# Sparse attention into an ELU layer on one core: another order for the opening, and the second batch's pieces from a list

## The chip, the core and the metric

The kernel runs on one core of one Trainium2 chip. A core has five instruction streams that run beside each other and meet only at semaphores: TensorE (PE, the matmuls; its weight loads are shown as PEld), VectorE (DVE), ScalarE (ACT), GpSimd (POOL) and SyncE (SP). Each engine takes its own instructions in the order in which the program issued them, so a piece that waits holds up what stands behind it on that engine. The metric is the device time of one execution in microseconds (us).

## What is computed

There are 8 batches of 8 heads, 576 positions and 64 values per head. The first four heads use a local mask (a query sees itself and the 31 positions before it), the other four a strided mask (a query sees earlier positions of the same residue modulo 32). The attention output, 4608 tokens of 512 values, goes through a two-layer feed-forward block with an ELU between.

```python
scores = scale * np.matmul(q, k.transpose(0, 1, 3, 2))
mask_local = (rel >= 0) & (rel < stride)
mask_strided = (rel >= 0) & (pos[None, :] % stride == pos[:, None] % stride)
...
h = x @ w_in                                   # 4608x512 @ 512x2048
g = np.where(h > 0.0, h, alpha * (np.exp(np.minimum(h, 0.0)) - 1.0))
return (g @ w_out).astype(np.float32)          # 4608x2048 @ 2048x512
```

## The kernel before

**Two streams of work, interleaved.** The feed-forward block works on chunks of 512 tokens, nine in all; attention works on batches of 576 tokens. Chunk 0 needs batch 0, chunk 1 needs all of batches 0 and 1, and so on. So batch 0 is computed first and almost alone (the *opening*), and from then on attention of batch nb+1 is cut into small pieces which are put between the matmuls of chunk nb.

**Attention pieces.** A batch has four pairs of heads: `s0`, `s1` (strided) and `l0`, `l1` (local). Capital `S0`, `S1` in the opening's list are the strided pairs of batch 1. A `Pair` has these pieces:

- `t_q`, `t_k`: TensorE transposes of q and k into a PSUM bank (L368 strided, 5 matmuls; L382 local, 12), and one copy of the bank to SBUF (L371, L385).
- `s0`, `s1` (scores, first and second half, L500: 4 or 6 matmuls into the double bank `pair_a`), followed by an exponential on ScalarE (L508) that gives the probabilities `pr`. In batches above 0 the mask multiplication on VectorE (L523) is issued right behind it; in batch 0 it is a piece of its own, `m0`, `m1`.
- `v`: a copy of the strided values into the layout with a column of ones (L421, two instructions). `halo`: a copy of the last 32 rows of each local value block (L428).
- `a0`, `a1`: probabilities times values (L542), then a reciprocal (L550) and a product (L551) on VectorE, which give the rows of `x`.
- `x`: transposes of `x` (L578 strided, L591 local) and a copy into `xT` (L585 and L587, or L595), from which the feed-forward matmuls read.

**Which engine copies.** `Pair.copy` takes ScalarE for batches 0 and 1, except, in batch 0, the steps named in `ON_VECTOR`. The halo of batch 1 is on VectorE.

**The opening.** `OPENING` is an order written out by hand. `fill.n` means n matmuls of 512 columns into a bank that nobody reads (L724). `moe.c` runs one quarter of the contraction for the first three tiles of chunk 0 (L629), so these three tiles are ready when the chunk begins. The attention and feed-forward banks are shared out by `Ring`s: `pair_a` for scores, three single banks for transposes and `a` pieces, and three banks (two halves and `single3`) for the tiles of chunk 0.

**A chunk.** For each of 16 steps s the loop runs the pieces of gap 2s, four matmuls into a bank (`moe_in`, L629), the ELU (`moe_act`), the pieces of gap 2s+1, and then an output part (`moe_out`, L678, four matmuls; a finished output of 128 rows is copied at L683 and stored). The ELU is an exponential on ScalarE (L655) and two VectorE instructions (L662, then L664, which reads the bank); for the steps in `ON_SCALAR` (4, 7, 10, 13, 15) of chunk 0 it is the exponential, a Relu on ScalarE (L658) and one VectorE instruction (L659). A bank comes free for the next tile when L664, or the Relu, has read it. In this document m3 means the four matmuls of step 3 of chunk 0, and so on to m15.

**The gaps of batch 1.** `attention(b, start, pitch, at)` places the pieces by a start, a pitch from pair to pair and eight offsets. For batch 1 these are `(3, 6, (-3, -2, 0, 2, 4, 6, 9, 3))`: a pair begins every six gaps, its scores come at 0 and 2, `a0` and `a1` at 4 and 6, and `x` at 9. The output parts of chunk 0 come behind m11, m13 and m15.

**Loads.** All loads of inputs are issued by GpSimd in program order; `w_in` comes in four quarters (512 columns each, four steps of a chunk each), then `w_out` in four.

Of the kernel before, what the change touches and what calls it, by code (L numbers as in the profile page):

```python
# [32 lines left out]
PIECES = (-2, -1, 0, 2, 3, 5, 7, 0)  # L33
TIMES = (
# [4 lines left out]
    ((2, 8, 15, 22), 0, PIECES),  # L39
)  # L40

OPENING = """
s0.cast_q s0.t_q s0.t_k s1.cast_q s1.t_k s0.s0 s0.m0 s1.t_q s0.s1 s0.m1 fill.2 l0.t_q s1.s1
s1.m1 s1.s0 s1.m0 l0.t_k l1.t_q fill.1 s0.v l0.s0 l0.m0 l1.t_k l0.s1 s1.a0 s0.a0 l0.m1 l1.s0
s1.a1 s0.a1 fill.1 l1.s1 l1.m0 fill.1 s1.halo s1.x fill.1 s0.x l1.m1 fill.1 l0.a0 fill.1 l0.a1
l1.a0 moe.2 l1.a1 S0.t_q l0.x S1.t_q moe.3 l1.x moe.0 moe.1
""".split()  # L50
ON_VECTOR = "s0.t_q s1.cast_q s1.t_k l0.t_q s0.v l1.x".split()


ON_SCALAR = (4, 7, 10, 13, 15)
# [4 lines left out]
def kernel(  # L59
# [55 lines left out]
    def share(sc, hps, ops, ring):  # L115
        rings.update(sc=Ring(*sc), hps=Ring(*hps), ops=Ring(*ops), ring=Ring(*ring))
# [71 lines left out]
    def load_local(b, name):  # L188
        if name == "v":

            nc.gpsimd.dma_start(
                out=v_loc[b % 3][32:128, :, :, :D].rearrange("p h i d -> p (h i) d"),
                in_=v[b, 0:4].rearrange("h (i p) d -> p (h i) d", p=LB))
            return
        flat = nat[name, "loc"][b % 3]
        if b < EARLY:
            nc.gpsimd.dma_start(
                out=flat[0:LB].rearrange("p (h x) -> p h x", h=4),
                in_=src[name][b, 0:4].rearrange("h (p j) d -> p h (j d)", j=L_RUN))
            return  # L200
        t = flat[:, 0:20 * D].rearrange("p (a i e d) -> p a i e d", a=2, i=5, d=D)
        for h in range(4):
            nc.gpsimd.dma_start(  # L203
                out=t[:, h // 2, 0:4, h % 2],
                in_=src[name][b, h, 0:512].rearrange("(i p) d -> p i d", p=128))
        for a in range(2):
            nc.gpsimd.dma_start(
                out=t[0:64, a, 4],
                in_=src[name][b, 2 * a:2 * a + 2, 512:576].rearrange("h p d -> p h d"))

    def transpose_batch(b, local):

        def strided():
            for name, to in (("q", qT), ("k", kT)):
                nc.sync.dma_start_transpose(out=to["str"][b % 2],
                                            in_=nat[name, "str"][b % 3])

        if BY_DMA <= b <= LATE and local < 2:
            strided()
        if b >= EARLY and local:  # L220
            for name, to, o in (("q", qT, 0), ("k", kT, 32)):
                for a in range(2):
                    nc.sync.dma_start_transpose(
                        out=to["loc"][b % 2][:, a, o:o + 640].rearrange(
                            "p (i r) -> p i r", r=128),
                        in_=nat[name, "loc"][b % 3][:, 640 * a:640 * a + 640])
        if b > LATE:
            strided()

    def load_batch(b):  # L230
        for name in "qkv":
            load_strided(b, name)
        for name in "qkv":
            load_local(b, name)
# [87 lines left out]
    def load_w_in(i):  # L322
        nc.gpsimd.dma_start(out=w_in_sb[:, :, 512 * i:512 * (i + 1)],
                            in_=wi[:, :, 512 * i:512 * (i + 1)])
# [5 lines left out]
    load_strided(1, "v")  # L330
    load_local(1, "q")
    load_local(1, "k")
    load_local(1, "v")
    load_w_in(2)


    class Pair:
# [6 lines left out]

        def copy(self, step, late):

            if self.b == 0:
                late = f"{self.name}.{step}" in ON_VECTOR
            return nc.vector.tensor_copy if late else nc.scalar.copy

        def cast(self, name):
# [214 lines left out]
        def x_out(self):  # L566
# [22 lines left out]
            else:  # L589
# [4 lines left out]
                        identity[0:LB, 0:LB])  # L594
                self.copy("x", self.b > 1)(dst, xt[:, 0:S])  # L595

    def attention(b, start, pitch, at):


        gaps = {}  # L600
        pairs = [Pair(b, s, hp) for s in (b < LATE, b >= LATE) for hp in range(2)]
        begin = [start + pitch * i for i in range(4)] if pitch else start
        if b >= LATE:
            gaps[begin[0]] = [pairs[3].halo]
        for i, pr in enumerate(pairs):
            if b == 1 and pr.strided:
                pr.t_q = lambda: None
            for off, piece in ((at[0], pr.t_q), (at[1], pr.t_k),
                               (at[7], lambda pr=pr: pr.v_in(0)),
                               (at[7] + (b > 1), lambda pr=pr: pr.v_in(1)),  # L610
                               (at[2], lambda pr=pr: pr.scores(0)),
                               (at[3] if b < WHOLE else at[2] + (b < LATE),
                                lambda pr=pr: pr.scores(1)),
                               (at[4], lambda pr=pr: pr.av(0)),
                               (at[5] - (b >= LATE and i == 0),
                                lambda pr=pr: pr.av(1)),
                               (at[6] + (b > 1 and pr.strided) + (b >= LATE), pr.x_out), (at[5] - 2, pr.halo if b < LATE else lambda: None)):
                gaps.setdefault(begin[i] + off, []).append(piece)
        return gaps
# [85 lines left out]
    def range_flag(row_ok16):  # L705
        cnt = rings["ring"].next()
        nc.tensor.matmul(cnt[0:1, 0:1], lhsT=row_ok16, rhs=ones, start=True, stop=True)
        nc.vector.tensor_scalar(flag, cnt[0:1, 0:1], scalar1=127.5, scalar2=None,
                                op0=ALU.is_le)

    def run(gaps, keys):
        for gap in sorted(g for g in gaps if g in keys):
            for piece in gaps[gap]:
                piece()

    every = range(-10, 1000)
    pairs = {p.name: p for p in (Pair(0, s, hp) for s in (True, False) for hp in range(2))}
    pairs.update((f"S{hp}", Pair(1, True, hp)) for hp in range(2))
    parts = [s for s in OPENING if s.startswith("moe")]
    for step in OPENING:  # L720
        pair, what = step.split(".")
# [29 lines left out]
    def outs(nb, s):  # L751

        if nb == 0:
            return [(0, i) for i in range(3) if s == 11 + 2 * i]
        step = [(nb - 1, i) for i in range(3, MC)]
        if nb < n_chunks:
            step += [(nb, i) for i in range(3)]
        else:
            step[0:2] = step[1::-1]
        return step[s:s + 1]  # L760

    for nb in range(n_chunks + 1):

        if nb + 1 < B:
            gaps = attention(nb + 1, *TIMES[min(nb + 1, 4)])
            if nb == 0:
                share([pair_a], b_halves + singles[3:], [], singles[:3])
            elif nb + 1 < LATE:
                share([pair_a], b_halves, singles[3:], singles[:3])
            else:  # L770
                share([pair_a], b_halves + singles[:1], singles[3:], singles[1:3])
        else:
            gaps = {}
            share([], b_halves + singles[:1], singles[2:], singles[1:2])
        if nb + 3 < B:
            load_batch(nb + 3)
        for s in range(MC):
            if nb == 0 and s == 10:
                share([pair_a], b_halves, singles[3:], singles[:3])
            if s == (9 if nb + 2 > LATE else 6) and nb > 0 and nb + 2 < B:  # L780
                transpose_batch(nb + 2, int(nb + 2 >= LATE))
            if s == 13 and nb + 2 == EARLY:
                transpose_batch(nb + 2, 2)
            run(gaps, (2 * s,) if s else range(-10, 1))
            late = LATE <= nb + 1 and s + 1 < MC
            if nb < n_chunks:
                moe_in(nb, s)
            if nb < n_chunks and not late:
                moe_act(nb, s)
            run(gaps, (2 * s + 1,) if s + 1 < MC else range(2 * s + 1, 1000))  # L790
            if nb < n_chunks and late:
                moe_act(nb, s)
            if nb == B and s == 4:
                range_flag(row_ok16)
            for chunk, i in outs(nb, s):
                moe_out(chunk, i)
        if nb + 1 == B:
            row_ok16 = range_check()
# [163 lines left out]
```

## Time and profile before

| | us |
|---|---|
| median of 3 runs (322.5 to 324.03) | 322.56 |
| the profiled execution | 322.0 |
| its span, first to last instruction | 320.2 |
| TensorE busy in the span | 299.3 (93%) |
| VectorE busy | 243.3 (76%) |
| ScalarE busy | 175.5 (55%) |

The span is 1.8 us shorter than the time of the same execution. Of the span, some 27 us are the opening; chunk 0 with batch 1 runs from there to about 55 us; the rest is chunks 1 to 8. A matmul of 512 columns is listed with 0.37 to 0.38 us, but four in a row start every 0.22 us: a listed duration holds the time until its result is out, and the issue of four takes 0.87 us.

### The profile page before, as it was taken

The page shows a single profiled execution, that of the slowest core. Times are in us where ns is not written, and L with a number is a line of the kernel's source. Part 1 is how long each engine was busy: PE and PEld are TensorE (multiplying, and loading weights), DVE is VectorE, ACT ScalarE, POOL GpSimd, SP SyncE. Part 2 cuts the span into 40 slices and gives each one's busy share as a digit, 9 for nine tenths or more (in the row PEclk, how much of TensorE's full clock was granted, in tenths as well). Part 3 has the DMA queues.
Part 4 walks back from the last instruction along what each step waited for, and adds up shares of the span by engine and source line. Part 5 has one row for each costly group of instructions (what it writes and reads, how often), then busy time and mean ns, then how long its engine had stood idle before and what let it go on. Part 6 is the DMA issues. An engine that isn't in the chain of part 4 may idle for free.

```text
span 320.2 us, 6034 instructions
## 1 busy us (share of the span) xinstructions
PE 299.3 (93%) x2173; PEld 150.3 (47%) x2214; DVE 243.3 (76%) x539; ACT 175.5 (55%) x334; POOL 138.3 (43%) x218
## 2 busy tenths in 40 slices
PE   1997888999999999999999999999999999999994
PEld 0564444445444544444444544444445444444443
DVE  6676987787878988988898879887988666776610
ACT  3668986777455555456655655555565444434411
POOL 9869615968957839958953920000000000000000
PEclk9999999999999999999999999999999999999998
DMA  6999999999999999999996992391111000110012
GB/s 106 166 182 121 181 207 127 151 140 176 96 149 168 142 128 208 88 136 176 210 148 86 158 200 58 88 147 49 53 51 35 34 33 35 52 47 34 35 68 73
DMA packets 108970, 36.33 MB, mean 113 GB/s; under 512 B 87357, under 2 KB 104453, under 8 KB 108933
## 3 DMA queue, kind: packets, MB, share of 16 engines
q0 software_dynamic: 71632, 18.10, 64.1%
q1 hardware_dynamic: 37301, 17.77, 28.4%
q8 instruction: 19, 0.31, 0.4%
q14 instruction: 18, 0.15, 0.2%
HBM read 36.70 MB, written 9.44 MB: 144 GB/s over the span
## 4 chain that ended last, share of the span: by engine, by line
PE 85%; DVE 6%; ACT 3%; issue 2%; DMA 2%; POOL 1%; ACTq 0%; POOLq 0%
PE single L678 38%; PE half L629 27%; PE single L629 9%; PE single L542 3%; PE pair_a L463 2%; DMA k_str<-in_k_dram 2%; DVE g_sb L664 2%; PE single L578 1%; DVE e_sb L662 1%; PE single L382 1%; PE pair_a L500 1%; DVE x_l L551 1%; ACT e_sb L655 1%; PE single L368 1%; PE single L724 1%
## 5 line engine op out<-in xcount | busy, mean ns | idle before, releaser
L678 PE MATMUL single<-w_out_sb,g_sb 128*128 128x512 bf16 (+1 forms) x576 | 144.0, 373 | 0.8
L629 PE MATMUL half<-xT,w_in_sb 128*128 128x512 bf16 x414 | 109.8, 379 | 1.2 <-issue 0.3
L655 ACT ACTIVATE e_sb<-half 128x512 f32<-128x512 f32 x109 | 65.4, 600 | 70.2 <-PE half L629 64.5
L662 DVE TENSOR_SCALAR e_sb<-e_sb 128x512 bf16<-128x512 f32 x139 | 62.7, 451 | 36.0 <-ACT e_sb L655 35.4
L678 PEld LDWEIGHTS <-g_sb 128*128 128x128 bf16 x592 | 54.7, 98 | 56.2
L629 PEld LDWEIGHTS <-w_in_sb 128*128 128x128 bf16 x576 | 52.2, 98 | 56.4 <-issue 0.6
L664 DVE TENSOR_TENSOR g_sb<-e_sb,half 128x512 bf16<-128x512 bf16 x104 | 71.6, 688 | 3.6
L629 PE MATMUL single<-xT,w_in_sb 128*128 128x512 bf16 x139 | 36.3, 379 | 0.4 <-DMA w_in_sb<-in_moe_w_in_dram 0.2
L655 ACT ACTIVATE e_sb<-single 128x512 f32<-128x512 f32 x35 | 21.0, 600 | 24.1 <-PE single L629 22.0
L683 ACT COPY o_sb<-single 128x512 f32<-128x512 f32 (+1 forms) x37 | 21.2, 574 | 17.1 <-PE single L678 16.5
L542 PEld LDWEIGHTS <-pr 128*128 128x128 bf16 (+3 forms) x352 | 20.7, 105 | 14.7 <-issue 1.0
L469 ACT ACTIVATE pr<-pair_a 126x936 bf16<-126x936 f32 (+1 forms) x20 | 19.2, 961 | 11.9 <-PE single L463 11.9
L664 DVE TENSOR_TENSOR g_sb<-e_sb,single 128x512 bf16<-128x512 bf16 x35 | 24.1, 688 | 1.2
L180 POOL DMA_DIRECT2D v_raw<-in_v_dram x32 | 20.2, 666 | 8.5 <-DVE v_str L421 5.6
L180 POOL DMA_DIRECT2D k_str<-in_k_dram x32 | 19.7, 632 | 7.8 <-issue 2.9
L180 POOL DMA_DIRECT2D q_str<-in_q_dram x28 | 17.3, 631 | 7.9 <-DMA w_out_sb<-in_moe_w_out_dram 2.0
L551 DVE TENSOR_TENSOR x_l<-single,rden 96x384 bf16<-96x384 f32 x32 | 17.7, 553 | 1.1
L203 POOL DMA_DIRECT2D q_loc<-in_q_dram x20 | 15.4, 797 | 3.6 <-PE half L629 1.5
L551 DVE TENSOR_TENSOR x_s<-single,rden 126x256 bf16<-126x256 f32 (+1 forms) x32 | 15.7, 491 | 1.1
L203 POOL DMA_DIRECT2D k_loc<-in_k_dram x20 | 15.3, 786 | 1.0 <-issue 0.8
L508 ACT ACTIVATE pr<-pair_a 128x576 bf16<-128x576 f32 (+2 forms) x20 | 13.0, 651 | 3.5 <-PE pair_a L500 3.4
L550 DVE RECIPROCAL rden<-single 96x6 f32<-96x6 f32 (+2 forms) x64 | 11.9, 186 | 3.0 <-PE single L542 2.6
(114 smaller groups left out, 256.4 us busy)
## 6 DMA issues: line engine op xcount, KB each, us to landing
out_dram<-o_sb SPq DMA_DIRECT2D x35, 256.0 KB, 2.7
v_loc<-in_v_dram POOLq DMA_DIRECT2D x8, 288.0 KB, 8.4
k_str<-in_k_dram POOLq DMA_DIRECT2D x32, 67.5 KB, 5.0
v_raw<-in_v_dram POOLq DMA_DIRECT2D x32, 67.5 KB, 5.1
w_in_sb<-in_moe_w_in_dram POOLq DMA_DIRECT2D x4, 512.0 KB, 9.5
w_out_sb<-in_moe_w_out_dram POOLq DMA_DIRECT2D x4, 512.0 KB, 17.0
q_str<-in_q_dram POOLq DMA_DIRECT2D x28, 67.5 KB, 7.4
q_loc<-in_q_dram POOLq DMA_DIRECT2D x20, 64.0 KB, 5.3
```

The lines of the kernel that those rows point to most:

```text
L180: engine.dma_start(out=t[0:108, h].rearrange("p g d -> p (g d)"), in_=rows[h, :, 0:30, :].rearrange("t (r g) d -> t r (g d)", g=5))
L203: nc.gpsimd.dma_start(out=t[:, h // 2, 0:4, h % 2], in_=src[name][b, h, 0:512].rearrange("(i p) d -> p i d", p=128))
L469: nc.scalar.activation(both, sc[0:nk, :, 0:w], ACT.Exp, scale=scale)
L508: nc.scalar.activation(halves, sc[0:nk, :, 0:w], ACT.Exp, scale=scale)
L542: nc.tensor.matmul(av[0:m, p, blk - b0, :], lhsT=pr[0:nk, o:o + m], rhs=vt[0:nk, 2 * self.hp + p, blk, :], start=True, stop=True)
L551: nc.vector.tensor_tensor(self.x[0:nq, b0:b0 + n].rearrange("q g p d -> q p g d"), av[0:nq, :, 0:n, 0:D], r.unsqueeze(3).to_broadcast([nq, ...
L629: nc.tensor.matmul(hps, lhsT=w_in_sb[:, c, m * 128:(m + 1) * 128], rhs=xT[:, c, nb * N_TILE:(nb + 1) * N_TILE], start=start, stop=stop)
L655: nc.scalar.activation(e_sb, hps, ACT.Exp)
L662: nc.vector.tensor_scalar(e1_sb, e_sb, scalar1=1.0, scalar2=1.0, op0=ALU.min, op1=ALU.subtract)
L664: nc.vector.tensor_tensor(g_of[nb][:, m, :], e1_sb, hps, op=ALU.max)
L678: nc.tensor.matmul(ops, lhsT=g_of[nb][:, m, kk * 128:(kk + 1) * 128], rhs=w_out_sb[:, m, cols], start=(m == 0), stop=(m == MC - 1))
L683: nc.scalar.copy(o_sb, ops)
```

## The change

It has these parts:

1. `OPENING` is reordered from `s0.a1` on. The halo goes ahead of the last local scores; `l0.a0` goes ahead of `l1.m1` and `s0.x`; two of the single `fill.1` go away (five after `s0.a1` become three); `S0.t_q` and `S1.t_q` go behind `moe.3` and to both sides of `l1.x`.
2. The copy of `S1.t_q` goes from ScalarE to VectorE.
3. Batch 1 is no longer placed by start, pitch and offsets but by the list `SECOND`, pairs of a gap and a step. `S0.s0` goes from gap 3 to 7, `S0.s1` from 5 to 9, and so on; the two scores of a strided pair overlap with the other pair's; `x` comes three or four gaps behind the pair's last values, where it was three; `l1.x` goes from gap 30 to 31. The masks of batch 1 stay behind their exponentials on VectorE.
4. The third quarter of `w_in` is issued ahead of the local values of batch 1 instead of behind them.
5. The output parts of chunk 0 come behind m12, m14 and m15; accordingly the third bank is handed from the tiles to the outputs at step 11 instead of 10.

```diff
-    (3, 6, (-3, -2, 0, 2, 4, 6, 9, 3)),
+    None,
...
+SECOND = """
+3 S0.t_k 7 S0.s0 8 S1.t_k 9 S0.s1 9 S0.v 11 S1.s0 11 S0.a0 12 S0.a1 13 S1.s1 14 S1.a0 14 l0.t_q
+16 S1.a1 16 S0.x 16 l0.t_k 18 l0.s0 19 S1.x 19 l1.t_q 20 S1.halo 20 l0.s1 21 l1.t_k 22 l1.s0
+23 l0.a0 24 l0.a1 24 l1.s1 26 l1.a0 27 l0.x 27 l1.a1 31 l1.x
+""".split()
...
-s1.a1 s0.a1 fill.1 l1.s1 l1.m0 fill.1 s1.halo s1.x fill.1 s0.x l1.m1 fill.1 l0.a0 fill.1 l0.a1
-l1.a0 moe.2 l1.a1 S0.t_q l0.x S1.t_q moe.3 l1.x moe.0 moe.1
+s1.a1 s0.a1 s1.halo fill.1 l1.s1 l1.m0 fill.1 s1.x l0.a0 l1.m1 fill.1 s0.x l0.a1 l1.a0 moe.2
+l1.a1 l0.x moe.3 S0.t_q l1.x S1.t_q moe.0 moe.1
 """.split()
-ON_VECTOR = "s0.t_q s1.cast_q s1.t_k l0.t_q s0.v l1.x".split()
+ON_VECTOR = "s0.t_q s1.cast_q s1.t_k l0.t_q s0.v l1.x S1.t_q".split()
...
     load_local(1, "k")
+    load_w_in(2)
     load_local(1, "v")
-    load_w_in(2)
...
-            if self.b == 0:
-                late = f"{self.name}.{step}" in ON_VECTOR
+            if self.b < 2:
+                name = self.name.upper() if self.b else self.name
+                late = f"{name}.{step}" in ON_VECTOR
...
+    def second():
+        pairs.update((f"l{hp}", Pair(1, False, hp)) for hp in range(2))
+        gaps = {}
+        for gap, step in zip(SECOND[::2], SECOND[1::2]):
+            pair, what = step.split(".")
+            gaps.setdefault(int(gap), []).append(
+                lambda p=pairs[pair], what=what: p.step(what))
+        return gaps
...
-            return [(0, i) for i in range(3) if s == 11 + 2 * i]
+            return [(0, i) for i in range(3) if s == (12, 14, 15)[i]]
...
-            gaps = attention(nb + 1, *TIMES[min(nb + 1, 4)])
+            gaps = attention(nb + 1, *TIMES[min(nb + 1, 4)]) if nb else second()
...
-            if nb == 0 and s == 10:
+            if nb == 0 and s == 11:
                 share([pair_a], b_halves, singles[3:], singles[:3])
```

More of the change, by code (lines that the diff above doesn't have):

```diff
@@ L605, in attention @@
         for i, pr in enumerate(pairs):
-            if b == 1 and pr.strided:
-                pr.t_q = lambda: None
             for off, piece in ((at[0], pr.t_q), (at[1], pr.t_k),
```

## The prediction, made before the changed kernel ran

> **What bounds the kernel now.** I read the slices of the page first, then the chain, then the TensorE, VectorE and ScalarE timelines between 17 and 57 us. In the page's slices TensorE stands at 9, that is 90% or more, from the eighth slice (56 us) on:
>
> ```profile
> span 320.2 us, 6034 instructions
> ...
> PE   1997888999999999999999999999999999999994
> ...
> DVE  6676987787878988988898879887988666776610
> ACT  3668986777455555456655655555565444434411
> ...
> PE 85%; DVE 6%; ACT 3%; issue 2%; DMA 2%; POOL 1%; ACTq 0%; POOLq 0%
> ```
>
> From there the order is the same in both kernels and TensorE has no gaps to give, so what counts is the moment at which chunk 1 starts: before, its first tile begins at 54.80 and its fourth matmul is issued by 55.67. What chunk 0 gains or loses goes straight to the end. TensorE's timeline shows the hand-over from the opening to chunk 0 and the worst waits behind it:
>
> ```profile
> 26.75 0.59 PE L629 MATMUL half<-xT,w_in_sb 128*128 128x512 bf16 x2
> 27.18 0.38 PE L629 MATMUL single<-xT,w_in_sb 128*128 128x512 bf16 x1
> 27.40 0.44 PE L368 MATMUL single<-identity,k_str 126*128 126x126 bf16 x5
> 28.61 0.28 PE L500 MATMUL pair_a<-qT_str,kT_str 64*128 64x126 bf16 x4 [0.78 <-ACT kT_str L371]
> 29.59 0.32 PE L500 MATMUL pair_a<-qT_str,kT_str 64*128 64x108 bf16 x6 [0.70 <-ACT pr L508]
> 29.84 1.04 PE L629 MATMUL half<-xT,w_in_sb 128*128 128x512 bf16 x4
> 31.36 0.31 PE L542 MATMUL single<-v_str,pr 126*128 126x65 bf16 x4 [0.48 <-ACT v_str L421]
> ...
> 52.94 0.30 PE L591 MATMUL single<-identity,x_l 96*128 96x96 bf16 x3 [0.80 <-DVE x_l L551]
> ```
>
> Three tiles end at 27.40. m3 needs a bank, and the first comes free at 29.54, when L664 of the first tile has read it; until then TensorE has S0's k transposes and scores, and waits between them. Issue times (five transposes 0.28, twelve 0.38, scores 0.22 to 0.25, `a` 0.15 or 0.21, four matmuls 0.87) and the starts of the rows give 6.9 us of waits between 27.40 and 54.80: 2.3 up to the first `a` piece, 0.6 and 0.9 for `x` of S0 and S1, 1.0 for `x` of l1, the rest in pieces under 0.5.
>
> VectorE's timeline shows the work that frees the banks, and one row that is not like the others:
>
> ```profile
> 26.24 0.46 DVE L595 COPY xT<-single 128x576 bf16<-128x576 bf16 x1 [1.50 <-PE single L591]
> 27.85 0.96 DVE L662 TENSOR_SCALAR e_sb<-e_sb 128x512 bf16<-128x512 f32 x1 [1.16 <-ACT e_sb L655]
> 28.85 0.69 DVE L664 TENSOR_TENSOR g_sb<-e_sb,half 128x512 bf16<-128x512 bf16 x1
> 29.46 0.42 DVE L662 TENSOR_SCALAR e_sb<-e_sb 128x512 bf16<-128x512 f32 x1
> ```
>
> L662 took 0.96 where it usually takes 0.42, while GpSimd wrote the descriptors of the local values (27.34 to 28.57). The first row is the copy for `l1.x`, after which `moe.1` could begin at 26.75.
>
> **The opening.** The steps that I use run from producer to consumer as the rows show: 0.22 us from the last matmul issued to the reader of its bank, 0.05 from a copy to TensorE. Before, the halo stands on ScalarE at 19.91 for 1.27 us, and both copies of `x`, to 22.33, stand behind it. Its load (issued at 10.11, landing after 7.9) is in at 18.0, and ScalarE is free at 18.2, so in the new order it runs from 18.2 to 19.5; the last local exponential slips from 19.24 to 19.43. `s0.x` is copied by 22.14 instead of 22.33, `moe.2` starts at 22.2 instead of 22.57. The larger part comes behind it: with `l0.a0` ahead of `l1.m1` the values of l1 are done at 24.05 instead of 24.73, and `l1.x`, which was issued behind `moe.3` at 25.71, goes to 24.24. `moe.0` and `moe.1` then follow without a gap, and the three tiles end at 26.07 instead of 27.40: 1.33 us earlier. The two fills that go away (0.41 each, in a stretch that is not waited for) are in this. `S1.t_q`'s copy on VectorE (0.47) lies in VectorE's idle 25.2 to 26.5; were that idle not there, it would put off the first L662 by 0.39. ScalarE, relieved of 0.58, waits for the first tile anyway until 25.9.
>
> **The list.** I walked the three engines in the new order, each instruction at the later of its engine and its inputs, with the durations of its row in the timelines. The first tile's exponential is at 25.90, its bank free at 27.67 if L662 takes 0.43. What filled the hole of TensorE now lies behind m3: only `S0.t_k` (0.28) is left, so TensorE waits 1.37 up to m3 at 27.72 (before: 29.84). Then:
>
> - m5 ends at 31.08, and `S1.s0` waits 1.0 for `pair_a`, since ScalarE does the exponential and Relu of m4 (0.50 and 0.48) ahead of the exponential of `S0.s1`, which ends at 32.06. Behind that the copy of `v` (1.36) keeps `S0.a0` and `a1` for 0.9, and the exponential of m5, which before ran ahead of it, until 33.21.
> - `S1.a0` waits 0.67 for its mask, which stands on VectorE behind L662 and L664 of m5; `l0.t_q` 0.41 for the bank that `S0.a0`'s product reads.
> - m7 ends at 37.17; `S1.a1` waits 0.92, since its mask stands behind two products of S0 (0.56 and 0.70) and the two instructions of m6 (1.05); `S0.x` waits 0.32 for a bank. m8 is at 39.26, before at 39.47: of 2.1 us of lead 0.2 is left.
> - `l1.t_k` and `l1.s0` stand in gaps 21 and 22 with nothing of the tiles between. The copy for `l1.s0` comes behind exponential and Relu of m10 and ends at 45.49, so TensorE waits 1.93 from 43.61. m11 is at 45.78, before at 45.30.
> - m14 waits 0.84 for the bank of m12, whose L664 comes behind both products of l0 and a mask. The wait for `l1.x` (1.0 before) is gone: it is issued behind m15 at 54.10, its product done at 53.46. Chunk 1's first three matmuls run from 55.21, the fourth waits 0.13 for the copy behind the Relu of m15, and is issued by 56.2.
>
> The waits add up to 8.8, with the gaps of 0.08 to 0.10 that the rows show between `a` or `x` pieces and what follows 9.1. Against 6.9 that is 2.2 more, less the 1.33 of the opening: +0.85. The walk itself ends 0.5 later than before, 0.7 with those gaps. I take **+0.8 us**.
>
> **Loads.** The two issues that change places both end on GpSimd at about the same time (0.88 and 1.23 us). The third quarter of `w_in` landed at 39.4 and m8 waited 0.25 for it; now 288 KB are no longer ahead of it, so it lands up to 2 us earlier. The wait at m8 is between 0 and 0.35; I take 0, since 39.26 is so close to the old landing that any advance covers it. The values land by some 40, and the halo runs at 43.4. The first output part needs the first quarter of `w_out` (44.5) at 48.2. What L662 can lose: the descriptors of the values now lie under the second or third L662 (rows of 0.79, 0.96 and 1.16 against 0.42), 0.4 to 0.7 on VectorE, hidden by ScalarE's copy of `v`; if not hidden it is the upper end. Durations are of the profiled execution, 322.0 with its 320.2 of span; that is 0.56 under the median, to which I add: 322.56 + 0.8 = 323.4.
>
> One page speaks against masks here. The Trainium skill (GPSIMD Engine Reference, Key points) says that GpSimd shares its SBUF interfaces with VectorE, in contention also with instructions of two SBUF inputs. By that the mask of `S1.s0`, which falls into GpSimd's memsets of 1.16 us (34.04 to 36.3), would be longer and `S1.a0` later, 0.4 by the row of 0.79, making +1.2. The trace disagrees: a mask at 35.48, inside the second memset, took 0.41 like all others, while the L662 behind it took 0.79.
>
> **The rivals.**
>
> *The list's waits come out smaller, and the opening's gain stays: faster.* It decides at VectorE: if the masks of `S1.s1` and the products pass ahead of the tiles' instructions (ScalarE late by one exponential is enough), the 0.92, 0.67 and 0.84 go, and 1.33 - (9.1 - 2.4 - 6.9) gives -1.5: 321.0. For it: before, the same masks cost TensorE only 0.6 in all. Against: the order on VectorE is fixed and it has 23 us of work from 26.5 to 51.
>
> *TensorE's clock rises one step later: slower.* Two matmul rows show it: five transposes take 0.69 at 20.43 and 0.44 at 23.42, and fills start 0.41 apart before 21.3 and 0.23 after. The page's granted clock reads 9 throughout, so durations are the evidence. With two fills less the change could come later; l1's pieces, `moe.2` and `moe.3` (2.8 us of issue in the next 3.4) would take up to 1.7 more, of which 0.4 is waiting anyway: +0.8 + 1.3 = 324.7. Against: the stretch 18.3 to 21.4 has no gap on TensorE in either order. The Trainium skill (TensorE: Matmul & The Clock Gate, Part 1) says that the clock doubles after a busy window of some 3.4 us, in windows that run freely; by that a lost window costs about the same, and the time would also scatter between executions.
>
> *ScalarE's backlog is worse than walked: slower.* From 41 to 46 ScalarE has no gap in my walk, and the wait of 1.93 grows by whatever is added ahead of `l1.t_k`'s copy; slow rows of L662 (0.4 to 0.7 each, up to three) add on VectorE. +0.8 + 1.2 = 324.6 if two of these show.
>
> **How the numbers follow.** About 0.5%, 1.6 us, is what a measurement of this kernel can tell from no change. The forecast, 323.4, own range 322.6 to 324.4: 0.46, nearly all within 0.5%. Faster rival 0.16, most of it around or past the bound. Clock 0.12 and backlog 0.26, most of both past it. So faster 0.14, same 0.46, slower 0.40. The range reaches from the faster rival to just beyond the slower ones: 321.1 to 325.3.
>
> **What would show it.** The three tiles end near 26.1 and m3 starts near 27.7; waits of about 1 us ahead of `S1.s0` and `S1.a1`, and nearly 2 ahead of `l1.s0` on ScalarE's k copy; no load wait at m8; chunk 1's first tile at 55.2 to 55.6; nothing changed behind it. The forecast is wrong if m3 is not early (the opening), if transposes at 22 to 24 us still take 0.69 (the clock), or if m8 to m11 is not where the lead goes (the list).

## The result and the profile after

The changed kernel takes 324.86 us (median of 16 runs, 322.43 to 327.74), the kernel before, run beside it, 322.83 us (16 runs, 321.89 to 324.78). The ratio is 1.0051 with a 95% interval of 1.0030 to 1.0072: slower, by 1.6 us by the ratio and 2.0 us by the medians. The slowest run, 327.74, is in a slower state and does not count in the ratio. Forecast was +0.8, or 323.4: the time went the way that was forecast and lies within the whole range (321.1 to 325.3), but above the forecast's own (322.6 to 324.4), where the two slower rivals stood (324.7 and 324.6). The profiled execution of the changed kernel took 324.1 us with a span of 322.3, against 322.0 and 320.2 before: 2.1 longer.

The code after has other line numbers for the same work: 7 more in the loads and memsets, 8 more in the attention pieces, 14 more in the tiles. The two VectorE instructions of a tile, L662 and L664, are now L676 and L678, and the mask, L523, is L531. From the page of the changed kernel, first the 40 slices, then the shares of the chain:

```profile
span 322.3 us, 6034 instructions
...
PE   1897679999999999999999999999999999999994
...
DVE  6687768687779988988798879887988566776610
ACT  3677775776545554555555665555555544434411
...
PEclk9999989999999999999999999999999999999999
...
PE 87%; DVE 4%; ACT 3%; issue 2%; DMA 2%; POOL 1%; ACTq 0%; POOLq 0%
```

TensorE's slices four to six (24 to 48 us) are 7, 6 and 7 where they were 7, 8 and 8, and the sixth slice of the granted clock shows 8. From the seventh on TensorE stands at 9 (before, from the eighth), VectorE and ScalarE read as before within one or two from there on, and the chain is still TensorE's, 87% of it. TensorE's timeline (start, busy time, work, and in brackets the wait ahead of it with its releaser) shows what the change does to chunk 0:

```profile
26.26 0.44 PE L376 MATMUL single<-identity,k_str 126*128 126x126 bf16 x5
27.93 1.02 PE L643 MATMUL half<-xT,w_in_sb 128*128 128x512 bf16 x4 [1.22 <-DVE g_sb L678]
...
32.27 0.29 PE L508 MATMUL pair_a<-qT_str,kT_str 64*128 64x126 bf16 x4 [0.64 <-ACT pr L516]
32.92 0.31 PE L550 MATMUL single<-v_str,pr 126*128 126x65 bf16 x4 [0.36 <-ACT v_str L429]
33.66 0.36 PE L550 MATMUL single<-v_str,pr 108*128 108x65 bf16 x6 [0.42 <-ACT v_str L429]
...
35.72 0.32 PE L550 MATMUL single<-v_str,pr 126*128 126x65 bf16 x4 [0.58 <-DVE pr L531]
...
38.55 0.38 PE L550 MATMUL single<-v_str,pr 108*128 108x65 bf16 x6 [0.86 <-DVE pr L531]
...
46.07 0.30 PE L508 MATMUL pair_a<-qT_loc,kT_loc 64*128 64x96 bf16 x6 [1.74 <-ACT kT_loc L393]
...
47.95 0.92 PE L550 MATMUL single<-v_loc,pr 128*128 128x65 bf16 x12
...
56.55 1.12 PE L643 MATMUL half<-xT,w_in_sb 128*128 128x512 bf16 x4
```

The three tiles end at 26.26 (before 27.40) and m3 starts at 27.93 (before 29.84), so the opening hands over 1.1 us and m3 comes 1.9 us sooner. Then come the waits for ScalarE (`pair_a`, the copy of `v`, the k copy of `l1` with 1.74) and for the masks; m11 is at 46.30 (before 45.30), and chunk 1 starts at 56.55 instead of 54.80: 1.75 late. The remaining 0.35 is lost behind that (from chunk 1's first tile to the end 265.75 against 265.40), where VectorE's timeline has one slow instruction of chunk 1's second tile, usually 0.42:

```profile
60.62 1.60 DVE L676 TENSOR_SCALAR e_sb<-e_sb 128x512 bf16<-128x512 f32 x1 [1.13 <-ACT e_sb L669]
```

One thing in the second half of this is no wait. The windows of the same profile (stretch, its length, busy time of the engines, then granted clock, DMA share and GB/s) show TensorE at half its clock right behind the 1.74:

```profile
43.00:46.36 3.36, 1.62 (x23) 0.75 (x24) 2.76 (x6) 3.01 (x7) 0.72 (x2) 1.00 1.24 209
46.37:49.78 3.41, 3.19 (x23) 1.76 (x25) 1.38 (x3) 1.76 (x3) 0.76 (x1) 0.50 1.24 205
49.79:56.00 6.21, 6.16 (x48) 3.32 (x48) 5.92 (x15) 3.21 (x7) 3.78 (x7) 1.00 0.99 125
```

In the first stretch TensorE was busy for 1.62 of 3.36 us. For the next 3.41 it got 0.50 of its clock, and the twelve `a` matmuls at 47.95 took 0.92 us, where they take 0.56 in executions in which the clock stays up. In the profile before, the clock stays up from 21.43 to the last 1.8 us of the span, in which TensorE has no work.

### The profile page after: what moved, and what is told of

It reads as the page before. It is cut to its first block, busy times and chain, and to the rows that moved or that the text cites. A ratio compares the mean times of both kernels' runs of the same rounds, so it can differ in the third digit from the quotient of the medians.

```text
span 322.3 us, 6034 instructions
## 1 busy us (share of the span) xinstructions
PE 300.2 (93%) x2171; PEld 150.8 (47%) x2212; DVE 243.7 (76%) x540; ACT 174.6 (54%) x333; POOL 140.2 (44%) x218
## 4 chain that ended last, share of the span: by engine, by line
PE 87%; DVE 4%; ACT 3%; issue 2%; DMA 2%; POOL 1%; ACTq 0%; POOLq 0%
PE single L692 37%; PE half L643 28%; PE single L643 9%; PE single L550 4%; PE pair_a L471 2%; DMA k_str<-in_k_dram 2%; PE pair_a L508 1%; PE single L586 1%; DVE g_sb L678 1%; PE single L390 1%; DVE e_sb L676 1%; ACT e_sb L669 1%; PE single L376 1%; DVE x_s L559 1%; PE single L599 1%
## 5 line engine op out<-in xcount | busy, mean ns | idle before, releaser
L643 PE MATMUL half<-xT,w_in_sb 128*128 128x512 bf16 x414 | 111.2, 382 | 2.6 <-DVE g_sb L678 1.2
L676 DVE TENSOR_SCALAR e_sb<-e_sb 128x512 bf16<-128x512 f32 x139 | 62.9, 453 | 37.3 <-ACT e_sb L669 36.6
L678 DVE TENSOR_TENSOR g_sb<-e_sb,half 128x512 bf16<-128x512 bf16 x104 | 71.5, 688 | 3.6
L678 DVE TENSOR_TENSOR g_sb<-e_sb,single 128x512 bf16<-128x512 bf16 x35 | 24.1, 688 | 1.2
L187 POOL DMA_DIRECT2D q_str<-in_q_dram x28 | 18.0, 660 | 6.4 <-DMA w_out_sb<-in_moe_w_out_dram 2.0
```

What stands on the lines that cost most here:

```text
L187: engine.dma_start(out=t[0:108, h].rearrange("p g d -> p (g d)"), in_=rows[h, :, 0:30, :].rearrange("t (r g) d -> t r (g d)", g=5))
L643: nc.tensor.matmul(hps, lhsT=w_in_sb[:, c, m * 128:(m + 1) * 128], rhs=xT[:, c, nb * N_TILE:(nb + 1) * N_TILE], start=start, stop=stop)
L676: nc.vector.tensor_scalar(e1_sb, e_sb, scalar1=1.0, scalar2=1.0, op0=ALU.min, op1=ALU.subtract)
L678: nc.vector.tensor_tensor(g_of[nb][:, m, :], e1_sb, hps, op=ALU.max)
```

## The experiments

All were timed in five rounds beside the kernel before, whose median was 323.34, 323.31 and 323.41 us in the three sets (35 runs each). The kernel before itself scatters from 321.1 to 327.3, so that ratios below have intervals of some 0.3% to each side, and each profile is one draw out of that scatter. "m3 to chunk 1" is the time between the starts of these tiles, 24.96 before and 28.62 after. The 28.62 holds the half-clock window; 27.85, used below, is an estimate without it. One profile of the changed kernel at full clock, with six memsets moved (below), shows 28.00.

### The opening alone

```diff
 # in the kernel before
-s1.a1 s0.a1 fill.1 l1.s1 l1.m0 fill.1 s1.halo s1.x fill.1 s0.x l1.m1 fill.1 l0.a0 fill.1 l0.a1
-l1.a0 moe.2 l1.a1 S0.t_q l0.x S1.t_q moe.3 l1.x moe.0 moe.1
+s1.a1 s0.a1 s1.halo fill.1 l1.s1 l1.m0 fill.1 s1.x l0.a0 l1.m1 fill.1 s0.x l0.a1 l1.a0 moe.2
+l1.a1 l0.x moe.3 S0.t_q l1.x S1.t_q moe.0 moe.1
-ON_VECTOR = "s0.t_q s1.cast_q s1.t_k l0.t_q s0.v l1.x".split()
+ON_VECTOR = "s0.t_q s1.cast_q s1.t_k l0.t_q s0.v l1.x S1.t_q".split()
```

> The opening's order and its copy on VectorE alone, on the kernel before; batch 1 by its old offsets, loads in their old order. By the prediction's first step the three tiles end at 26.1 to 26.3 instead of 27.40. Theory A, the gain is kept by the old list: 1.3 us faster. Theory B, the third quarter of w_in (39.4 before, needed at m8) is what the old list then runs into: m8 waits some 1.0 to 1.2 for it and no more than 0.3 is left. I expect B, 0 to 0.4 faster.

Measured: 322.89 us, ratio 0.9975 (0.9942 to 1.0009). m3 is at 29.05, 0.79 sooner than before. In the profile that lead met a load, in TensorE's timeline at m8:

```profile
41.13 1.11 PE L630 MATMUL single<-xT,w_in_sb 128*128 128x512 bf16 x4 [2.71 <-DMA w_in_sb<-in_moe_w_in_dram]
```

m8 waited 2.71 us for the third quarter of `w_in`, more than the 1.0 to 1.2 expected, and the clock was at half from 41.96 to 45.38. So in this profile chunk 1 came at 57.01, 2.2 us later than before. The runs are not slower, so a wait of that size is probably not in all of them. The gain of the opening alone is 0.8 us by the ratio, and its interval reaches zero.

### The opening, and the load's place too

```diff
 # in the kernel before, with the opening above
-    load_local(1, "v")
     load_w_in(2)
+    load_local(1, "v")
...
-(at[5] - 2, pr.halo if b < LATE else lambda: None)
+(9 if b == 1 else at[5] - 2, pr.halo if b < LATE else lambda: None)
```

The second edit puts batch 1's halo into gap 18, behind the later landing of the values.

> As the opening alone, with the third quarter of w_in ahead of the local values of batch 1, and the halo of batch 1 put from gap 13 to gap 18 so that it does not stop VectorE at a load that now lands near 40.6. Theory B of the opening alone gives a time about 1.0 to 1.3 us under the kernel before. If the opening is worth nothing at the end (theory: what it gains is given back anywhere in chunk 0), no difference.

Measured: 323.25 us, ratio 0.9985 (0.9950 to 1.0020). The wait at m8 is gone (m8 at 38.87, before 39.47). Now an `a` piece of l0 waits for the halo, in TensorE's timeline:

```profile
43.44 0.30 PE L543 MATMUL single<-v_loc,pr 128*128 128x65 bf16 x4 [0.59 <-DVE v_loc L429]
```

Chunk 1 starts at 55.01, no sooner than before. The halo did not wait for its transfer, which had landed by 41.5 (issued at 29.7, 11.5 us to landing); it ran at 42.90, right behind a mask on VectorE. So what costs here is the halo's later gap, chosen because of the load, and not the load. With the gaps of before, neither order of the two loads kept the earlier opening's lead.

### The list alone

The changed kernel with the opening, the copy of `S1.t_q` and the order of the loads as before:

```diff
 # in the changed kernel: OPENING and ON_VECTOR as before, and
-    load_w_in(2)
     load_local(1, "v")
+    load_w_in(2)
```

> The list and the later output parts alone, on the old opening and the old order of loads. By the walk the list costs 2.1 us against the old offsets at m11 and chunk 1's start, without the opening's 1.3 to set against it: 2 us slower if only waits count. If the wait of nearly 2 us ahead of l1.s0 also lowers TensorE's clock for one window of 3.4 us, as the trace of the changed kernel shows at 46.4 to 49.8, 2.5 to 4 us slower, with times that scatter by more than 2 us.

Measured: 326.29 us, ratio 1.0070 (1.0038 to 1.0102), so 2.3 us slower. Together with the 0.8 that the opening alone gave, that makes 1.5, and the changed kernel loses 1.6: the parts add up, within intervals of about 1 us each, and the list is what costs. The profile has the waits of the changed kernel (1.74 ahead of `l1.s0`, m3 to chunk 1 28.40), one of them longer (`S1.a0` 1.19, behind an L676 of 1.09), no clock drop, and a loss behind chunk 1's start of 1.05 us, to which I come with the memsets.

### Filling the long wait

```diff
 # in the changed kernel's list
-20 l0.s1 21 l1.t_k 22 l1.s0
+20 l0.s1 21 l1.t_k 21 fill.7 22 l1.s0
```

A `fill.7` is seven matmuls that nobody reads; they keep TensorE busy in the wait ahead of `l1.s0` and leave everything else where it is.

> The changed kernel with seven matmuls of 512 columns into an unread bank between l1.t_k and l1.s0, where TensorE waits 1.8 us. They take 1.5 us of that wait and should end before l1.s0 can start. Theory, clock: the half rate at 46.4 to 49.8 goes, the time falls by 1.0 to 1.4 us to about 0.3 us over the kernel before, and the scatter shrinks. Rival, the wait itself is what costs: no change against the changed kernel, or a little slower.

Measured: 324.57 us, ratio 1.0034 (0.9998 to 1.0070). The profile's clock stays up, as the window behind the filled wait shows:

```profile
46.40:49.70 3.30, 3.30 (x35) 1.80 (x31) 1.97 (x5) 2.50 (x4) 0.58 (x1) 1.00 1.24 204
```

From m11 to chunk 1 takes 9.42 us here, 10.25 in the changed kernel with its half-clock window: the drop costs 0.8 us where it falls, with a wait of 0.68 ahead of m14 gone in the slower stretch. The list alone, which had the same 1.74 us wait and no fill, kept its clock and also took 9.42. So the wait does not drop the clock each time: in the list alone it fell into one window of 3.41 us, busy for 0.49, and no drop followed. Where it falls in these windows also differs from execution to execution; with the memsets moved (below), two windows shared it, busy for 0.87 and 0.62. The fill's gain over the changed kernel, 0.17% by the ratios, can't be told from nothing, and the scatter did not shrink (322.55 to 327.37).

### `l1.s0` behind m11

```diff
-20 l0.s1 21 l1.t_k 22 l1.s0
-23 l0.a0 24 l0.a1 24 l1.s1 26 l1.a0 27 l0.x 27 l1.a1 31 l1.x
+20 l0.s1 21 l1.t_k
+23 l0.a0 23 l0.a1 23 l1.s0 25 l1.s1 26 l1.a0 27 l0.x 28 l1.a1 31 l1.x
```

> The changed kernel with l1.s0 behind m11 and both l0 value pieces instead of directly behind l1.t_k (l1.s1 and l1.a1 one gap later). The wait of 1.8 us ahead of l1.s0 shrinks to some 0.5, since m11 and the two pieces (1.3 us) need nothing of it. Theory: this wait is the largest single loss of the list, so chunk 1 starts 0.7 to 1.3 us earlier, and the half rate that follows it does not come. Rival, VectorE is what sets chunk 1's start: the waits move on to m13 and m14 and no more than 0.3 us is gained.

Measured: 324.08 us, ratio 1.0024 (0.9993 to 1.0056). In TensorE's timeline the 1.74 has become 0.37, and a new wait stands behind it:

```profile
47.40 0.30 PE L508 MATMUL pair_a<-qT_loc,kT_loc 64*128 64x96 bf16 x6 [0.37 <-ACT kT_loc L393]
50.83 0.37 PE L550 MATMUL single<-v_loc,pr 128*128 128x65 bf16 x6 [0.95 <-DVE pr L531]
```

`l1.a0` waits 0.95 for its mask, because the scores come two gaps later. m3 to chunk 1 is 26.93, 0.9 less than the 27.85 estimated for the changed kernel without its clock drop, 1.1 less than the 28.00 measured.

### The kernel before, with the two pieces next to each other

```diff
 # in the kernel before
-            for off, piece in ((at[0], pr.t_q), (at[1], pr.t_k),
+            for off, piece in ((at[0], pr.t_q),
+                               (at[2] if b == 1 and i == 3 else at[1], pr.t_k),
```

> The kernel before with one piece moved: l1.t_k from gap 19 to gap 21, directly ahead of l1.s0. If the neighbourhood of the two is what makes the wait, TensorE waits some 1.2 us for the copy behind exponential and Relu of m10, m11 goes from 45.3 to near 46.8, and chunk 1 starts 1.0 to 1.5 us later. Rival, the kernel has slack behind m11 that takes it up: less than 0.4 us.

Measured: 323.29 us, ratio 1.0015 (0.9987 to 1.0042). The neighbourhood alone makes the wait: 1.14 us ahead of `l1.s0`, m11 1.1 and chunk 1 0.75 later than in the profile before. The 0.75 lies between the theory's 1.0 to 1.5 and the rival's 0.4. The wait is smaller than the list's 1.74, probably because less of ScalarE's work waits at that moment in the kernel before, and the runs don't resolve its cost.

### No masks in batch 1

```diff
 # in the changed kernel
-            if self.b:
+            if self.b > 1:
```

> The changed kernel without the eight mask multiplications of batch 1, so the output of batch 1 is not the reference's; 2.9 us of VectorE's work goes and nothing is put in its place. Theory: the waits ahead of S1.a0, S1.a1 and m14 (0.6, 0.9 and 0.7 or more) are the masks' place in VectorE's order; chunk 1 starts 1.5 to 2 us earlier than in the changed kernel, at or ahead of the kernel before. Rival, ScalarE's order sets these times and the masks only fill gaps: 0.5 us or less.

Measured: 323.99 us, ratio 1.0022 (0.9996 to 1.0048). With the masks of batch 1 left out, `S1.a0` (0.58) and `S1.a1` (0.86) wait no more, but others take their place in TensorE's timeline:

```profile
37.07 0.45 PE L390 MATMUL single<-identity,q_loc 96*64 96x96 bf16 x12 [0.49 <-DVE x_s L559]
39.74 0.41 PE L586 MATMUL single<-identity,x_s 126*128 126x126 bf16 x5 [1.04 <-DVE x_s L559]
46.71 0.30 PE L508 MATMUL pair_a<-qT_loc,kT_loc 64*128 64x96 bf16 x6 [1.74 <-ACT kT_loc L393]
```

The products of `x` now end last, and the 1.74 is what it was (as is the half clock behind it, 47.78 to 51.19). m3 to chunk 1 is 27.93 against 28.62: of 1.44 us of waits, 0.7 goes. In the profiles the masks on VectorE are a part of the cost, and not the larger one. The ratios don't rank them: without the masks the kernel gains 0.29% on the changed one, by `l1.s0` behind m11 0.27%.

### The copy of the values of S0 on VectorE

```diff
 # in the changed kernel
-ON_VECTOR = "s0.t_q s1.cast_q s1.t_k l0.t_q s0.v l1.x S1.t_q".split()
+ON_VECTOR = "s0.t_q s1.cast_q s1.t_k l0.t_q s0.v l1.x S1.t_q S0.v".split()
```

This takes 1.36 us out of ScalarE's queue, at the place that the following lines of the changed kernel's ScalarE timeline show: the exponential of m5 (33.51) stands behind the copy (32.24).

```profile
31.48 0.74 ACT L516 ACTIVATE pr<-pair_a 108x648 bf16<-108x648 f32 x1
32.24 1.36 ACT L429 COPY v_str<-v_raw 126x512 bf16<-126x512 bf16 x2
33.51 0.59 ACT L669 ACTIVATE e_sb<-single 128x512 f32<-128x512 f32 x1
```

> The changed kernel with the copy of batch 1's strided values on VectorE (0.8 us there, in a gap of 1.36) instead of ScalarE (1.36 us, ahead of m5's exponential). If ScalarE's order around m4 and m5 is what gives the lead away, m5's exponential starts 1.2 us earlier, m8 goes from 39.8 to near 39.0 and chunk 1 starts 0.5 to 1.0 us earlier. Rival, the wait ahead of l1.s0 takes it up: 0.2 us or less.

Measured: 323.79 us, ratio 1.0036 (1.0004 to 1.0067). m3 to chunk 1 is 26.88, again some 1.0 less than 27.85, and chunk 1 starts at 54.08, 0.7 sooner than before, in an execution whose three tiles also ended early, at 25.54. But from there to the end it takes 266.5 where before took 265.4. VectorE waits 2.27 us for values of batch 2, which comes back below with the memsets.

### Both edits together

The two edits above in one kernel.

> The changed kernel with two edits together: the copy of the values of S0 on VectorE, and l1.s0 behind the values of l0. Theory (the list's cost in chunk 0 is ScalarE's order, in two separate places): each edit alone took some 0.9 to 1.0 us off the stretch from m3 to chunk 1 (27.85 without a stretch at half clock), so both together give 25.9 to 26.1; with m3 at 27.2 to 27.9 chunk 1 starts at 53.2 to 54.0, about 1 us ahead of the kernel before (54.80). Behind chunk 1's start up to 0.5 us is lost to VectorE, so the time is 0.3 to 0.8 us under the kernel before: ratio 0.9975 to 0.999. Rival (the two waits lie on one chain, and the second edit gains nothing once the first is made): 26.8, chunk 1 at 54.4, ratio 1.000 to 1.002.

Measured: 323.84 us, ratio 1.0009 (0.9985 to 1.0033), against 1.0051 for the changed kernel: 0.4% or 1.4 us better, level with the kernel before, and not faster than it. So the number is the rival's. The profile doesn't show the rival's reason for it. m3 waits 1.71 in this execution, behind an L676 of 0.91 for the first tile, and a stretch at half clock follows (35.15 to 38.56), and chunk 1 starts at 55.88. VectorE's timeline then shows, in chunk 1's second tile, the instruction L676, usually 0.42, with 2.85 us:

```profile
57.66 0.43 DVE L676 TENSOR_SCALAR e_sb<-e_sb 128x512 bf16<-128x512 f32 x1 [0.90 <-ACT e_sb L669]
...
59.95 2.85 DVE L676 TENSOR_SCALAR e_sb<-e_sb 128x512 bf16<-128x512 f32 x1 [1.13 <-ACT e_sb L669]
```

and GpSimd's timeline what ran meanwhile:

```profile
59.60 1.32 POOL L198 DMA_DIRECT2D v_loc<-in_v_dram  x1
60.77 0.48 POOL L257 MEMSET q_loc<- 32x256 bf16 x1
...
62.03 0.48 POOL L257 MEMSET k_loc<- 32x256 bf16 x1
```

L676 ended at 62.80, 0.29 behind the last of the six memsets. In four more profiles it ended 0.27 to 0.29 behind the last of them: the changed kernel (1.60 long), the list alone (2.71), with the fill (2.02) and `l1.s0` behind m11 (2.20). It is not so each time. In the kernel before (1.16 long), with the opening alone and with `l1.t_k` moved (1.09 each) the instruction began beside the descriptors of `v_loc` too, but ended 0.25 to 0.28 behind them, while the memsets went on. What decides between the two stays open. The Trainium skill (SBUF — State Buffer, Who interferes with whom) calls the port pair that VectorE and GpSimd share an exclusive lock, held for a whole instruction, the loser blocked. The runs agree with that, and show more: the loser can wait not for one instruction but for a run of seven that follow each other closely.

### The memsets ahead of batch 2's loads

```diff
-    load_batch(2)
     for i in range(3):
         clear_loc(i, nc.gpsimd)
+    load_batch(2)
```

This was done to three kernels: both edits together, the changed kernel, and the kernel before.

> As the combination, and GpSimd's six memsets of the local q and k buffers run ahead of the loads of batch 2 (at about 37 us) instead of behind them (60.2 to 61.9). Theory (the time lost behind chunk 1's start, 0.2 to 1.1 us, is a tile's VectorE instruction made slow by descriptors and memsets of GpSimd): with the memsets gone from there that instruction takes 0.4 to 1.2 us instead of 2.0 to 2.7, and from chunk 1's first tile to the end takes 265.4 to 265.7, like the kernel before (265.40), against 266.2 to 266.7 in the combination: ratio 0.996 to 0.998. Rival (the descriptors alone do it, or it is something else): no difference to the combination.

> The changed kernel, its list as it is, with the six memsets alone moved ahead of the loads of batch 2. Theory (GpSimd's memsets beside chunk 1's second tile): from chunk 1's first tile to the end 265.4 to 265.6 instead of 265.76 to 266.7, time 0.2 to 0.6 us shorter than the changed kernel: ratio to the kernel before 1.003. Rival (they cost nothing, or the loads of batch 2, issued 1.7 us later, are late for chunk 1): ratio 1.005 as the changed kernel, or above, with waits of TensorE on a DMA in chunk 1.

> The kernel before with the six memsets alone moved ahead of the loads of batch 2. In its profile the tile's instruction at 58.78 took 1.16 us and TensorE did not wait for it. Theory: nothing to gain, ratio 0.999 to 1.001, with 265.3 to 265.5 from chunk 1's first tile to the end. Rival (the memsets cost the kernel before too, in the executions whose loads are slower): ratio 0.997 to 0.999.

Measured: 324.00 us, ratio 1.0021 (0.9992 to 1.0050) for both edits together; 324.85, 1.0048 (1.0024 to 1.0072) for the changed kernel; 323.61, 1.0000 (0.9971 to 1.0029) for the kernel before. The long L676 is gone from the profiles of the two changed kernels (0.49 and 0.43), which agrees with the memsets making it; in the kernel before it takes 1.16 beside the descriptors, as it did with the memsets in their old place. But no ratio moves by what can be measured: 1.0009 to 1.0021, 1.0051 to 1.0048, and 1.0000. Either the slow instruction costs little in most executions, or what it gives back goes to the loads of batch 2, which now stand 1.6 to 1.9 us of memsets later in GpSimd's queue; these runs don't tell which. In the profile of the changed kernel with this edit, from chunk 1's first tile to the end takes 265.4 us, as in the kernel before, and that execution, which also had no clock drop, comes out at a span of 321.0.

With both edits and the memsets moved, m3 to chunk 1 is 26.21 (0.42 of it a load wait at m8, and nearly the 25.9 to 26.1 expected), chunk 1 starts at 54.07, 0.73 sooner than before, and then VectorE's timeline has this:

```profile
63.48 0.29 DVE L429 COPY v_str<-v_raw 126x512 bf16<-126x512 bf16 x1 [3.85 <-DMA v_raw<-in_v_dram]
63.69 0.41 DVE L531 TENSOR_TENSOR pr<-pr,mask_w 126x504 bf16<-126x504 bf16 x1
64.02 0.42 DVE L676 TENSOR_SCALAR e_sb<-e_sb 128x512 bf16<-128x512 f32 x1
```

The copy of batch 2's values stands on VectorE ahead of a tile's L676 and waits 3.85 us for its load. The copies of finished outputs, from the second behind chunk 1's start on, are 2.3 us later, measured from that start, than in the kernel before. The loads of batch 2 are issued by GpSimd, which waits for earlier loads to land between its issues. In that profile:

```profile
46.32 0.57 POOL L187 DMA_DIRECT2D q_str<-in_q_dram  x1 [1.97 <-DMA w_out_sb<-in_moe_w_out_dram]
...
54.10 0.59 POOL L191 DMA_DIRECT2D k_str<-in_k_dram  x1 [2.12 <-DMA w_out_sb<-in_moe_w_out_dram]
...
55.81 1.27 POOL L187 DMA_DIRECT2D v_raw<-in_v_dram  x2
```

None of these issues waits for chunk 1, so an earlier chunk 1 doesn't get its values any sooner (the first of `v_raw` is issued at 54.12 in the kernel before). In the two executions in which chunk 1 started before the 54.80 of the kernel before, at 54.08 and 54.07, the 0.7 us won were given back in full: behind chunk 1's start 1.1 and 2.6 us more passed than before. Of the 2.6, 2.3 are lost by the second output copy, where the late values are; of the 1.1 it is 0.5, and the rest goes later in small steps, the largest of them behind an L676 of 1.10 us at 84.56.

## Why the prediction was right, and where it was short

**The opening.** The three tiles end at 26.26 and not 26.07, since the halo waited 0.25 for its load (18.62 instead of 18.2) and the clock came up at 22.47 (before 21.43), so that matmuls at 21.39 still ran slow. In the memset variant of the changed kernel, the clock was up at 20.70 and the tiles end at 25.91. Over all profiles the end swings far more, with the moment at which the clock rises and with drops in the opening: 25.54 to 27.59 in the ten with the new order, 27.32 to 28.40 in the four with the old one. Their means, 26.4 and 27.8, differ by 1.4, so the step is right (1.33 forecast); that single profiles came within 0.2 of 26.07 is in part luck.

**The list.** Its waits are where they were put: ahead of m3 1.22 (1.37 forecast), `S1.s0` 0.64 (1.0), the two `a` pieces of S0 0.78 (0.9), `S1.a0` 0.58 (0.67), `l0.t_q` 0.22 (0.41), `S1.a1` 0.86 (0.92), `l1.s0` 1.74 (1.93). `S0.x` waits about 0.2 (0.32), m14 0.68 in the profiles at full clock (0.84). The causes are the ones given, as the profiles of the edits show: ScalarE's order (two edits, some 1.0 us each), and less the masks (0.7). By the ratios these three edits gain 0.27%, 0.15% and 0.29%, too close for their intervals to rank them. One wait swings: `S1.a0` waited 1.19 and 1.16 in the profiles of the list alone and of the fill, in which m5's L676 (L684 in the kernel with the fill), ahead of its mask on VectorE, took 1.09 and 1.05 instead of 0.42.

**The sum at full clock** can be read from the changed kernel with its memsets moved, whose clock held and whose L676 was not slow. From the end of the three tiles at 25.91 to chunk 1 at 55.57 it took 29.66, before 27.40: the list costs 2.26, where the waits were put at 2.2. Chunk 1 is 0.77 late and the span 321.0, 0.8 longer than before, the forecast's +0.8. It is one execution, and not the usual one: it and one more of that kernel's twelve runs had a mean granted clock of 1.000 and took 322.79 and 322.88, the other ten 324.55 to 326.69.

**What was left out** is the other 1.3 us of the changed kernel's profiled execution: 0.35 from an opening in which the clock rose late, 0.63 between the tiles' end and chunk 1 (30.29 against 29.66), which the half-clock window of 46.37 to 49.78 accounts for, and 0.33 behind chunk 1's start, where L676 took 1.60. Three sentences of the prediction failed there. The clock's rival was weighed only for the rise in the opening, and the prediction did not ask what the waits that the list adds would do to the clock, the largest of them 1.74 of a window of 3.41 us. "Nothing changed behind it" was wrong, as the later start put a VectorE instruction of chunk 1 among GpSimd's memsets. And slow L662 rows were taken for hidden by ScalarE's copy in chunk 0; there they were small in this profile (0.48 and 0.54) but, as just said, not hidden in two others, and in chunk 1 one row of 1.60 was not covered.

**In the medians** the kernel lost 1.6 to 2.0 us and not 0.8. The forecast's terms came from one execution of the kernel before, in which the clock held and no such row cost TensorE anything; the typical execution of the changed kernel carries the extra. The fill (324.57) and the moved memsets (324.85) each take one part of it away in the profile, and neither moves the ratio by more than the measurement tells. The mean granted clock on record with each run says more; one window of 3.41 us at half clock lowers it by 0.005. Of the 27 runs that count for the changed kernel, with its memsets in either place, 21 have 0.995 or less and a median of 325.0, and six have more and take 323.5. Of the 103 of the kernel before beside the experiments, 42 have 0.995 or less (323.8) and 61 more (323.1). So at a clock that held the changed kernel is only some 0.5 us behind, though by few runs, and most of what the medians add comes with a lower clock, which it has in four runs of five and the kernel before in two of five. This is a correlation over separate sets of runs: a long wait for something else also lowers the clock, so VectorE's and the loads' share in it stays open. What moves it is to take out the waits themselves: from 1.0051 to 1.0024 and 1.0036 with one edit each, and to 1.0009 with both (1.0021 when their memsets are moved too); the intervals of the single edits still overlap with that of the changed kernel.

**Loads.** m8 did not wait, as forecast. Where it came earlier, at 39.10 with both edits and the memsets moved, it waited 0.42, a little more than the bound of 0.35; the 2.71 of the opening alone came with the old order of the loads. Of the opening's 1.33 the runs of that kernel show 0.8, with an interval that reaches zero.

**The rivals.** The faster one asked that the masks and products pass ahead of the tiles' instructions on VectorE; they did not. Its supporting number, 0.6 us that the masks cost before, does not show in the profile before: no wait of TensorE in chunk 0 is put down to a mask there. The two profiles in which chunk 1 did start early, by 0.7, gave it back, one of them mostly to the values of batch 2. The later clock showed in part (the rise at 22.47), and the clock came back as a cost where it was not looked for. ScalarE's backlog was, if anything, less than walked; the slow rows of L662, the other half of that rival, came as said.

**The rule of the Trainium skill** that spoke against masks (GPSIMD Engine Reference, Key points) fares as it did in the trace of before: a mask at 35.25, inside a memset of 34.81 to 35.97, took 0.41. What suffers is the tile's L676, which reads one SBUF input in 32-bit floats.

## What to carry to other kernels

A walk through three engine queues by hand gave this list's cost to 0.1 us of what one profile at full clock shows, and that profile is not the usual execution; what it missed were side effects of the waits that it had itself found. When a change adds a wait of half a clock window to TensorE, price the drop that can follow (0.8 us here) as well as the wait, and ask of each later instruction that shifts what it will now stand beside on another engine. When an early stage is made faster, look first at the loads behind it: here the opening alone met one at m8, and an earlier chunk 1 met the values of batch 2.

## What the runs showed of the hardware

TensorE's clock fell to half for one window of 3.41 us (two in one profile) behind windows of that length in which it was less busy, but not idle throughout. Worked out from the matmul rows in the same free phase, the windows ahead of a drop were busy for 0.24 (the opening alone), 0.49 (the changed kernel, and without masks), 0.51 (both edits), 0.55 (S0's values on VectorE, in the opening) and 0.61 (`l1.s0` behind m11, in the opening). Windows of 0.49 (the list alone), 0.55 (the kernel before) and 0.58 (with the fill) were followed by none. So between 0.49 and 0.61 either can follow, and no window of these profiles up to 70 us that was busier was followed by a drop; what else counts stays open. In the profile with two slow windows the clock stayed down for the second although the first was 0.95 busy. The first rise came between 13.1 and 23.9 us. The Trainium skill (TensorE: Matmul & The Clock Gate, Part 1) puts the fall to half clock behind an idle window of about 3.4 us. The length and the free phase agree; the runs differ on idle, as shown.

A VectorE instruction of 0.42 us took up to 2.85 us beside GpSimd. It ended 0.27 to 0.29 us behind the last of six memsets in five profiles, and 0.25 to 0.28 behind the descriptors, ahead of the last memsets, in three.
